# A routed-expert kernel: splitting one store, and working off two early tiles of the first expert instead of one

## The chip, the cores and the metric

The kernel runs on 1 core of a Trainium2 chip, as one launch. The metric is device microseconds (us) for one execution. The core has five engines that each work through their own instructions in order and wait for one another by semaphores: TensorE (PE, matrix products; PEld is its weight load), VectorE (DVE), ScalarE (ACT), GpSimd (POOL) and SyncE (SP). SP, ACT and POOL also issue DMA transfers, which 16 DMA engines carry out.

## The reference

Three layers follow each other, all in float32:

- Attention for 4 batches, 8 heads, head width 64, with 512 local and 32 global tokens per batch. Local queries see a window of 32 positions to either side and the global keys; global queries see everything. The result has 2176 rows (4 x 544) of 512 numbers.
- A dense layer on these rows: `h = x @ w_in` (512 to 2048), `relu(h)` squared, `@ w_out` (back to 512).
- A routed layer: a row is worked on if `x @ w_skip > 0`. It goes to one expert of 8, the `argmax` of `x @ w_gate`, and its result is `x + gate * (relu(x @ w1[e]) @ w2[e])`, with `gate` the softmax probability of that expert. `w1[e]` is 512 x 1024 and `w2[e]` 1024 x 512. Other rows are copied.

## The kernel before, in words

**Tokens.** The 2176 rows are worked in 17 tiles of 128: 16 tiles of local tokens, and a last tile that holds the global tokens of all four batches (32 rows each). A row of the dense layer's result goes twice to DRAM: to `out`, and to a scratch tensor `x2d` that carries the row's gate as a 513th number. `store` (line 551) does it. For a local tile both targets are one block of 128 rows. For the last tile the target is four blocks of 32 rows that lie 544 rows apart, and one DMA to each target writes all four.

**Routing.** `route` (line 573) takes a tile in five steps (between its `yield`s): transpose the rows on PE and copy them on ACT; split them in three bfloat16 parts (`thirds`, three DVE operations); logits on PE, then the arg max, a long run of small DVE operations, and an exponential on ACT; rank the tokens within their expert (PE and some fifteen DVE operations, of which the second writes the gate into the row; for the last tile the store is issued right behind it, from SP); write the token's row number into a table of slots with a PE product and a DVE addition. Each expert has 17 columns of 128 slots in that table, one column per tile of its tokens. `slot_rows` (line 756) turns columns of the table into the row numbers that `gather` (line 821) reads and the scatter at the end of an expert's tile writes.

**Closing.** Before the last three tiles are routed (14 of 17 done), the kernel takes column 0 of expert 0 as final: it converts that column and raises expert 0's count to at least 128 (lines 982 to 985), so that later tokens go to later columns.

**An expert's tile.** `gather` fetches 128 rows of `x2d` by an indirect DMA from POOL. `prepare` (line 827) transposes them on PE (4 transposes) and splits them in a high and a low part (ACT, DVE). `expert_tile` (line 833) then has ten steps: four with 6 products each for the hidden layer, the third of which also turns the first half of the hidden values (4 transposes on PE, a cast on ACT, a subtraction on DVE); four with 6 products each for the output, the first of which turns the second half; one DVE operation that scales and adds; and the scatter, an indirect DMA from POOL.

**Weights.** An expert's weights come in 8 parts of 512 KB. `fetch_expert` (line 775) issues a part's DMA from SP, or from ACT where told; `convert_expert` (line 787) splits it in two halves (a cast on ACT, a subtraction on DVE or POOL). Parts are fetched up to 13 ahead.

**The order.** All engines' programs are written in the order in which the Python code emits them. `TAIL` (line 41) is that order by hand for the end of the dense layer and the start of the experts:

- `T`: the next step of the dense layer's last tile. `r`, `s`, `t`: a routing step of the last two local tiles and of the tile of global tokens.
- `O`: gather for tile 0 of expert 0, from the closed column. `pEJ`, `gEJ`: prepare, gather for tile J of expert E.
- `X`: the next step of tile 0 of expert 0. `S`: all columns of the table are converted, the counts copied.
- `w`, `W`: fetch the next weight part, from SP or from ACT. `C`, `c`: convert the next part, with DVE or POOL for the low half.

Behind `TAIL` come two more gathers and the scatter of expert 0's tile 0 (lines 1039 to 1042). Then, for every expert, its tile 0 is emitted with the weight traffic of the next expert, the counts are read into registers on every engine, and `more` (line 1048) emits tiles 1 to 4 in nested branches that are entered if the count is large enough. Before a tile is worked in such a branch the gather of the tile behind it is issued, and it is prepared after the sixth step.

Of the kernel before, what the change touches and what calls it, by code (L numbers as in the profile page):

```python
# [11 lines left out]
I32 = mybir.dt.int32  # L12
U32 = mybir.dt.uint32
AF = mybir.ActivationFunctionType
ALU = mybir.AluOpType
# [23 lines left out]
"""  # L39

TAIL = """
    w T T r T r r s T T s T s W r w T T r T s C C T c s w T T T C W O W T c C W T p00 C w C T w W T W W X t C
    X t t C X t c X t w w S g01 g10 X w w X w w X w p01 p10 X X
"""

WARM = 8
# [3 lines left out]
def attention_ffn_routed_experts(  # L50
# [499 lines left out]

    def store(t, x2, queue):

        globals_of = [d.rearrange("(b s) d -> b s d", b=B)[:, 0:SG, :] for d in (x2d, out)]
        if t < NLT:
            b, tt = divmod(t, TPB)
            r0 = b * S + SG + tt * P
            queue.dma_start(x2d[r0:r0 + P, :], x2)
            queue.dma_start(out[r0:r0 + P, :], x2[:, 0:DM])
        if t in (0, NLT):

            queue.dma_start(globals_of[0], x2)
        if t == NLT:
            queue.dma_start(globals_of[1], x2[:, 0:DM])

    w27 = []

# [150 lines left out]
    def ffn_tile(t):  # L717

        xh, xl = xts.pop("g")
        acc = ps.tile([P, DM], F32, tag="x2", bufs=2, name=f"acc{t}")  # L720
        gs = []
        for fb in range(N5):
            h = ps.tile([P, 512], F32, tag="h", bufs=2, name=f"h{t}_{fb}")
            for k in range(KD):
                w = w_in_t[k, fb]
                nc.tensor.matmul(h, lhsT=xh[:, k, :], rhs=w[:, 0, :], start=(k == 0), stop=False)
                nc.tensor.matmul(h, lhsT=xh[:, k, :], rhs=w[:, 1, :], start=False, stop=False)
                nc.tensor.matmul(h, lhsT=xl[:, k, :], rhs=w[:, 0, :], start=False, stop=(k == KD - 1))
                if k == 1:
                    yield  # L730
            g = sb("vr", 6, [P, ROW], f"g{t}_{fb}")[:, 0:512]
            square_relu(g, h)
            gs.append(g)
            yield
        for fb in range(N5 + 1):
            if fb < N5:
                tr = pair(f"gtr{t}_{fb}")
                transposes(tr, gs[fb])
                gh = sb("vr", 6, [P, ROW], f"gh{t}_{fb}")[:, 0:512].rearrange("p (a k) -> p a k", a=4).bitcast(F32R)
                gl = sb("pT", 2, [P, 4, P], f"gl{t}_{fb}").bitcast(F32R)  # L740
                split(gh, gl, tr)
                gs[fb] = (gh, gl)
            if fb:
                gh, gl = gs[fb - 1]
                for z in range(4):
                    f = 4 * (fb - 1) + z
                    wh, wl = wout(f)
                    nc.tensor.matmul(acc, lhsT=gh[:, z, :], rhs=wh, start=(f == 0), stop=False)
                    nc.tensor.matmul(acc, lhsT=gh[:, z, :], rhs=wl, start=False, stop=False)
                    nc.tensor.matmul(acc, lhsT=gl[:, z, :], rhs=wh, start=False, stop=(f == KF - 1))  # L750
                    if z % 2:
                        yield
        outs["g"] = (t, copy_out(t, acc))


    def slot_rows(gi, si, c0, c1):

        t = table[:, c0:c1]
        tmp = sb("ohs", 1, [P, NSLOT], f"slots{c0}_{c1}")[:, c0:c1]
        nc.vector.tensor_scalar(out=gi, in0=t, scalar1=-1.0, scalar2=0.0, op0=ALU.add, op1=ALU.max)  # L760
        nc.vector.tensor_scalar(out=tmp, in0=t, scalar1=0.0, scalar2=BIG, op0=ALU.is_equal, op1=ALU.mult)
        nc.vector.scalar_tensor_tensor(out=si, in0=tmp, scalar=-1.0, in1=t, op0=ALU.add, op1=ALU.add)
# [58 lines left out]
    def gather(e, j, gi):  # L821
        nc.gpsimd.indirect_dma_start(  # L822
            out=gathered(e, j), out_offset=None, in_=x2d, in_offset=bass.IndirectOffsetOnAxis(ap=gi, axis=0),
            bounds_check=NTOK - 1, oob_is_err=False,
        )

    def prepare(e, j):
        tr = pair(f"etr_{e}_{j}")
        transposes(tr, gathered(e, j))
        x = prepared(e, j)  # L830
        split(x[:, 0], x[:, 1], tr)
# [66 lines left out]
    with tc.manual_schedule():  # L898
# [54 lines left out]
        warm(WARM)  # L953
        for what in SEQ.split():
            do(what)
        first_slots = const.tile([P, 1], I32, name="g0"), const.tile([P, 1], I32, name="s0")
        rest_on[0] = nc.gpsimd
        for j in range(2, NB):
            emit = attention_block(j + 1) if j + 1 < NB else None
            ra, rb = outs.pop(j - 1)  # L960
            route_gens = {"r": route(*ra), "s": route(*rb)}
            ffn, unit, routed = ffn_block(j), -1, 0
            for what in (ODD if j % 2 else EVEN).split():
                if what in "FE":
                    square_on[0] = nc.vector if what == "F" else nc.scalar
                    next(ffn)
                    unit += 1
                    if j < NB - 1:
                        continue
                    if unit == 4:  # L970
                        xts["g"] = tuple(sb(n, 2, [P, KD, BLK], f"{n}_g", F32R)[:, :, 0:P] for n in ("xh", "xl"))
                        split(*xts["g"], xgT)
                    if unit == 16:
                        for n in range(FIRST):
                            fetch_expert(n, nc.sync)
                elif what in route_gens:
                    next(route_gens[what])
                    routed += 1
                    if j == NB - 1 and routed == 10:


                        slot_rows(*first_slots, 0, 1)
                        nc.vector.tensor_scalar(
                            out=count[:, 0:1], in0=count[:, 0:1], scalar1=float(P), scalar2=None, op0=ALU.max
                        )
                elif what == "V":
                    do(what)
                elif emit and what not in "rs":
                    emit(what)
# [5 lines left out]
        def slot(idx, e, j):  # L995
            c = e * TPE + j
            return idx[:, c:c + 1]

        route_gens = dict(zip("rs", (route(*o) for o in outs.pop(NB - 1))))
        ffn, tile00 = ffn_tile(NLT), None  # L1000
        fetched, converted = [FIRST], [0]
        for what in TAIL.split():
            if what == "T":
                next(ffn, None)
            elif what == "X":
                if tile00 is None:
                    tile00 = expert_tile(0, 0, first_slots[1])
                next(tile00)
            elif what in "rst":
                if what not in route_gens:  # L1010
                    route_gens[what] = route(*outs["g"])
                next(route_gens[what])
            elif what in "Cc":
                convert_expert(converted[0], nc.vector if what == "C" else nc.gpsimd)
                converted[0] += 1
            elif what in "Ww":
                fetch_expert(fetched[0], nc.scalar if what == "W" else nc.sync)
                fetched[0] += 1
            elif what == "O":
                open_places()  # L1020
                gather(0, 0, first_slots[0])
            elif what == "S":
                slot_rows(gidx, sidx, 0, NSLOT)
                nc.vector.tensor_copy(cnt, count)
            elif what[0] in "gp":
                e, j = map(int, what[1:])
                gather(e, j, slot(gidx, e, j)) if what[0] == "g" else prepare(e, j)

        def work(e, u):

# [8 lines left out]
        for u in AHEAD:  # L1039
            for n, j in AHEAD[u]:  # L1040
                gather(n, j, slot(gidx, n, j))
        next(tile00, None)

        def hint(e, j):

# [25 lines left out]
        for e in range(E):  # L1071
            for u, _ in enumerate(expert_tile(e, 0, slot(sidx, e, 0)) if e else ()):
                if u == 0:
                    hint(e, 1)
                if u == U1:
                    prepare(e, 1)
                if u == U0 and e + 1 < E:
                    prepare(e + 1, 0)
                work(e, u)
            if n_tok is None:  # L1080
                n_tok = [
                    nc.values_load(
                        cnt[0:1, i:i + 1], min_val=0, max_val=NTOK,
                        skip_runtime_bounds_check_because="a count of tokens, from 0 to all of them",
                    )
                    for i in range(E)
                ]
            more(e, 1)


# [28 lines left out]
```

## Time and profile before

| what | value |
|---|---|
| median of 3 runs | 785.13 us (784.14 to 787.31) |
| profiled execution | 787.99 us, of which the span from first to last instruction 786.3 us |
| mean granted TensorE clock | 0.972 of full |
| PE busy | 745.4 us (95%) |
| DVE, ACT, POOL busy | 427.2 us (54%), 395.4 us (50%), 175.2 us (22%) |

All times of the profile are microseconds from the span's start. The profile's views used below are: stretches (busy time of each engine in a window, with the number of its instructions, the granted TensorE clock and the share of the 16 DMA engines that is busy); waits (an engine's waits by what ended them: sum, number, longest); the timeline of an engine (start, length, operation; in brackets the idle time before it and what ended it); the summary of one line; the SP queue's timeline (when DMAs were issued). Busy matmuls overlap, so a step from one start to the next is the time that a product costs. A line ending in q (SPq, ACTq) is the issuing of a DMA or another instruction of that engine's sequencer, not its work.

### The profile page before, as it was taken

The page shows a single profiled execution, that of the slowest core. Times are in us where ns is not written, and L with a number is a line of the kernel's source. Part 1 is how long each engine was busy: PE and PEld are TensorE (multiplying, and loading weights), DVE is VectorE, ACT ScalarE, POOL GpSimd, SP SyncE. Part 2 cuts the span into 40 slices and gives each one's busy share as a digit, 9 for nine tenths or more (in the row PEclk, how much of TensorE's full clock was granted, in tenths as well). Part 3 has the DMA queues.
Part 4 walks back from the last instruction along what each step waited for, and adds up shares of the span by engine and source line. Part 5 has one row for each costly group of instructions (what it writes and reads, how often), then busy time and mean ns, then how long its engine had stood idle before and what let it go on. Part 6 is the DMA issues. An engine that isn't in the chain of part 4 may idle for free. (4 is left out here: it accounts for less than half of the span.)

```text
span 786.3 us, 16840 instructions
## 1 busy us (share of the span) xinstructions
PE 745.4 (95%) x6547; PEld 613.7 (78%) x6547; DVE 427.2 (54%) x1109; ACT 395.4 (50%) x972; POOL 175.2 (22%) x211
## 2 busy tenths in 40 slices
PE   6889999999999999999999999999885999999897
PEld 4666677888888888888888888887654877887775
DVE  2877984954641641662552663332781178417882
ACT  5774665566345544544654543433360268426771
POOL 5000121231211112111211111221222133313421
PEclk8598999999999999999999999999998999999999
DMA  9899470250425024142313031002458179516700
GB/s 265 222 318 273 104 185 7 58 132 28 105 55 125 28 45 88 33 128 63 78 45 95 2 118 51 5 28 80 146 191 292 55 249 326 194 53 243 272 25 30
DMA packets 117270, 95.21 MB, mean 121 GB/s; under 512 B 83005, under 2 KB 90173, under 8 KB 117164
## 3 DMA queue, kind: packets, MB, share of 16 engines
q1 hardware_dynamic: 107640, 73.17, 33.1%
q10 hardware_dynamic: 6644, 12.33, 4.3%
q0 software_dynamic: 2880, 8.33, 3.1%
q8 instruction: 62, 1.02, 0.5%
q14 instruction: 44, 0.36, 0.1%
HBM read 82.08 MB, written 12.85 MB: 121 GB/s over the span
## 5 line engine op out<-in xcount | busy, mean ns | idle before, releaser
L178 POOL TENSOR_TENSOR gl<-g,gh 128x256 fp32r<-128x256 f32 x107 | 78.8, 736 | 343.0 <-ACT gh L177 191.4
L669 PE MATMUL h<-xh,w_in 128*128 128x256 f32 x448 | 131.7, 294 | 0.0
L671 PE MATMUL h<-xh,w_in 128*128 128x256 f32 x448 | 126.6, 283 | 0.0
L670 PE MATMUL h<-xl,w_in 128*128 128x256 f32 x448 | 126.3, 282 | 0.0
L673 ACT ACTIVATE g<-h 128x256 f32<-128x256 f32 x128 | 48.8, 381 | 105.8 <-PE h L671 66.3
L690 PE MATMUL acc<-w_out,gh 128*128 128x512 f32 x224 | 93.4, 417 | 0.0
L692 PE MATMUL acc<-w_out,gl 128*128 128x512 f32 x224 | 88.3, 394 | 0.0
L691 PE MATMUL acc<-w_out,gh 128*128 128x512 f32 x224 | 88.1, 393 | 0.0
L669 PEld LDWEIGHTS h<-xh,w_in 128*128 128x128 f32 x448 | 84.7, 189 | 3.5
L670 PEld LDWEIGHTS h<-xl,w_in 128*128 128x128 f32 x448 | 84.6, 189 | 1.8
L671 PEld LDWEIGHTS h<-xh,w_in 128*128 128x128 f32 x448 | 84.4, 188 | 0.0
L410 ACT ACTIVATE sm<-sm,mx 128x128 f32<-128x128 f32 x128 | 49.9, 391 | 61.7 <-DVE mx L408 59.2
L177 ACT CAST gh<-g 128x256 fp32r<-128x256 f32 x112 | 45.4, 406 | 25.9 <-DVE g L703 23.7
L703 DVE TENSOR_TENSOR g<-h,g 128x256 f32<-128x256 f32 x44 | 18.5, 420 | 58.1 <-ACT g L673 58.0
L692 PEld LDWEIGHTS acc<-w_out,gl 128*128 128x128 f32 x224 | 42.1, 188 | 10.0 <-POOL gl L178 0.2
L178 DVE TENSOR_TENSOR ehl<-ertr,ehl 128x512 fp32r<-128x512 f32 x28 | 19.4, 691 | 52.9 <-ACT ehl L177 52.9
L690 PEld LDWEIGHTS acc<-w_out,gh 128*128 128x128 f32 x224 | 42.2, 188 | 6.8 <-ACT gh L177 0.4
L691 PEld LDWEIGHTS acc<-w_out,gh 128*128 128x128 f32 x224 | 42.3, 189 | 5.7 <-issue 0.3
L853 ACT ACTIVATE er<-eh 128x512 f32<-128x512 f32 x28 | 16.7, 597 | 38.7 <-PE eh L850 38.7
L688 PE MATMUL acc<-st_raw_out,gh 128*128 128x512 f32 x64 | 33.6, 649 | 0.0
L822 POOL DMA_INDIRECT xg<-x2d,slots x21 | 23.5, 1121 | 43.7 <-DVE xp L178 8.6
L890 POOL DMA_INDIRECT out_dram<-eo,slots x13 | 16.5, 1269 | 71.5 <-DVE eo L886 39.7
(706 smaller groups left out, 1681.9 us busy)
## 6 DMA issues: line engine op xcount, KB each, us to landing
st_e<-in_moe_w_dram SPq DMA_DIRECT2D x57, 512.0 KB, 8.0
vr<-in_v_l_dram SPq DMA_DIRECT2D x56, 192.0 KB, 3.7
st_raw_in<-in_moe_w_in_dram SPq DMA_DIRECT2D x16, 512.0 KB, 7.3
st_raw_out<-in_moe_w_out_dram SPq DMA_DIRECT2D x16, 512.0 KB, 5.4
x2d<-x ACTq DMA_DIRECT2D x17, 256.5 KB, 2.8
st_gv<-in_v_l_dram SPq DMA_DIRECT2D x8, 512.0 KB, 6.8
out_dram<-x ACTq DMA_DIRECT2D x16, 256.0 KB, 3.0
st_e<-in_moe_w_dram ACTq DMA_DIRECT2D x7, 512.0 KB, 5.5
```

The lines of the kernel that those rows point to most:

```text
L177: nc.scalar.copy(hi, src)
L178: (lo_engine or nc.vector).tensor_tensor(out=lo, in0=src, in1=hi.bitcast(F32), op=ALU.subtract)
L410: nc.scalar.activation(sm[:, hh, :], sm[:, hh, :], AF.Exp, bias=mx[:, hh:hh + 1], scale=SCALE, accum_out=osum[:, 2 * hh + g:2 * hh + g + 1],)
L669: nc.tensor.matmul(h, lhsT=wh, rhs=xh[:, k, :], start=(k == 0), stop=False)
L670: nc.tensor.matmul(h, lhsT=wh, rhs=xl[:, k, :], start=False, stop=False)
L671: nc.tensor.matmul(h, lhsT=wl, rhs=xh[:, k, :], start=False, stop=(k == KD - 1))
L673: nc.scalar.activation(g, h, AF.Relu)
L688: nc.tensor.matmul(acc[z], lhsT=gh[:, c], rhs=w, start=(f == 0), stop=(f == KF - 1))
L690: nc.tensor.matmul(acc[z], lhsT=gh[:, c], rhs=wh, start=(f == 0), stop=False)
L691: nc.tensor.matmul(acc[z], lhsT=gh[:, c], rhs=wl, start=False, stop=False)
L692: nc.tensor.matmul(acc[z], lhsT=gl[:, c], rhs=wh, start=False, stop=(f == KF - 1))
L822: nc.gpsimd.indirect_dma_start(out=gathered(e, j), out_offset=None, in_=x2d, in_offset=bass.IndirectOffsetOnAxis(ap=gi, axis=0), bounds_ch ...
```

## The change

Three things change.

- `store`: the last tile's one DMA to `x2d` and one to `out` become four each, one per block of 32 rows, the four to `x2d` first.
- Two columns of expert 0 are closed in place of one (the count is raised to at least 256). `O` issues both gathers. A letter `Y` is new: a step of expert 0's tile 1. `p01` moves up to the end of the dense layer's last tile. All ten steps of tile 0 (`X`) stand between the routing steps of the last tile and right behind `S`; the steps of tile 1 (`Y`) follow. The branch for tile 1 is gone: `more` starts at tile 2 for expert 0.
- Behind `S` the gathers are those for tile 2 of expert 0 and tile 0 of expert 1; the scatter of tile 0 is issued behind them, inside `TAIL`. The seven last fetches of `TAIL`, which SP issued before, are issued by ACT, between the steps `Y`.

```diff
-    w T T r T r r s T T s T s W r w T T r T s C C T c s w T T T C W O W T c C W T p00 C w C T w W T W W X t C
-    X t t C X t c X t w w S g01 g10 X w w X w w X w p01 p10 X X
+    w T T r T r r s T T s T s W r w T T r T s C C T c s w T T T C W O W T c C W T p00 C w C T p01 w W T W W X X
+    t C X t X t C X X t c X X X t S g02 g10 X Y Y Y W W Y W W p02 p10 Y W W Y Y W Y Y Y Y
...
-        globals_of = [d.rearrange("(b s) d -> b s d", b=B)[:, 0:SG, :] for d in (x2d, out)]
...
-        if t in (0, NLT):
-
-            queue.dma_start(globals_of[0], x2)
+        if t == 0:
+
+            queue.dma_start(x2d.rearrange("(b s) d -> b s d", b=B)[:, 0:SG, :], x2)
         if t == NLT:
-            queue.dma_start(globals_of[1], x2[:, 0:DM])
+
+            for d, n in ((x2d, ROW), (out, DM)):
+                for b in range(B):
+                    queue.dma_start(d[b * S:b * S + SG, :], x2[b * SG:(b + 1) * SG, 0:n])
...
-                        slot_rows(*first_slots, 0, 1)
+                        slot_rows(*first_slots, 0, 2)
                         nc.vector.tensor_scalar(
-                            out=count[:, 0:1], in0=count[:, 0:1], scalar1=float(P), scalar2=None, op0=ALU.max
+                            out=count[:, 0:1], in0=count[:, 0:1], scalar1=2.0 * P, scalar2=None, op0=ALU.max
...
-            elif what == "X":
-                if tile00 is None:
-                    tile00 = expert_tile(0, 0, first_slots[1])
-                next(tile00)
+            elif what in "XY":
+                j = "XY".index(what)
+                if j not in early:
+                    early[j] = expert_tile(0, j, first_slots[1][:, j:j + 1])
+                next(early[j], None)
...
-                gather(0, 0, first_slots[0])
+                for j in range(2):
+                    gather(0, j, first_slots[0][:, j:j + 1])
...
-        next(tile00, None)
...
-            more(e, 1)
+            more(e, 1 if e else 2)
```

## Rows read from the trace of the kernel before

**Rows 1.** The page: PE busy in tenths, in 40 slices of the span.

```profile
PE   6889999999999999999999999999885999999897
```

**Rows 2.** Stretches: length, busy (instructions) of PE, PEld, DVE, ACT, POOL; clock, DMA share, GB/s.

```profile
595.00:600.00 5.00, 0.00 (x0) 0.00 (x0) 0.00 (x0) 0.00 (x0) 3.83 (x4) 0.94 1.03 388
...
646.50:660.00 13.50, 13.21 (x64) 10.52 (x64) 11.73 (x13) 11.03 (x15) 5.22 (x4) 1.00 0.99 334
```

**Rows 3.** Stretches, PE alone: length, busy (instructions); clock, DMA share, GB/s.

```profile
575.90:607.57 31.67, 18.85 (x85) 0.84 0.68 230
607.57:620.16 12.59, 12.59 (x60) 1.00 0.17 57
...
584.00:585.70 1.70, 1.70 (x8) 0.50 0.00 0
```

**Rows 4.** Waits of PE from 560 us on: sum, times, longest.

```profile
PE etr L272 <- DMA xg<-x2d,slots: 8.4, 2, 7.8
PE pt L645 <- DVE ohl L642: 3.7, 2, 1.9
...
PE pl L591 <- DVE x2T L570: 1.4, 1, 1.4
```

**Rows 5.** Timeline of PE: start, length, operation, [idle before, releaser].

```profile
574.07 0.60 PE L272 MATMUL etr<-ident,xg 128*128 128x128 f32 x4
574.42 0.48 PE L748 MATMUL acc<-w_out,gh 128*128 128x512 f32 x1
...
602.05 1.09 PE L272 MATMUL etr<-ident,xg 128*128 128x128 f32 x4 [7.78 <-DMA xg<-x2d,slots]
...
607.57 0.49 PE L848 MATMUL eh<-e0h,xp 128*128 128x512 f32 x1 [0.65 <-issue]
...
618.77 0.39 PE L863 MATMUL y<-e7h,ehl 128*128 128x512 f32 x1
...
620.16 0.39 PE L848 MATMUL eh<-e0h,xp 128*128 128x512 f32 x1
```

**Rows 6.** Timeline of the SP queue.

```profile
587.57 0.65 SPq L561 DMA_DIRECT2D x2d<-x  x1
...
588.96 47.23 SPq L785 DMA_DIRECT2D st_e<-in_moe_w_dram  x14
```

**Rows 7.** DMA queues from 589.5 to 590.5: packets, MB, share of 16 engines.

```profile
q1 hardware_dynamic: 9, 0.02, 25.5%
```

**Rows 8.** Lines 557 (store of a local tile) and 822 (gather), ns and us.

```profile
L557 ACTq DMA_DIRECT2D x2d<-x x16: 327/332/376, 158.5 to 562.2; - x16
DMA to landing us min/median/max: 2.6/2.8/3.1
...
DMA to landing us min/median/max: 3.5/4.2/6.9
```

**Rows 9.** Timeline of POOL.

```profile
595.25 1.01 POOL L822 DMA_INDIRECT xg<-x2d,slots  x1 [7.70 <-DMA x2d<-x]
...
607.99 1.02 POOL L890 DMA_INDIRECT out_dram<-eo,s  x1 [7.81 <-DVE eo L886]
612.08 1.03 POOL L822 DMA_INDIRECT xg<-x2d,slots  x1 [3.07 <-DMA out_dram<-eo,s]
```

**Rows 10.** Timeline of DVE, the last tile's routing.

```profile
587.15 0.14 DVE L618 TENSOR_SCALAR rt<-rt 128x1 f32<-128x1 f32 x1
...
588.86 0.34 DVE L642 TENSOR_SCALAR ohl<-iota_s,rt 128x128 fp32r<-128x128 f32 x1
...
589.96 0.23 DVE L760 TENSOR_SCALAR slots<-table 128x136 int32<-128x136 f32 x1
```

**Rows 11.** Issues of line 785 (weight fetches), ns, and SP's longest wait there, us.

```profile
L785 SPq DMA_DIRECT2D st_e<-in_moe_w_dram x57: 367/462/1542, 456.2 to 738.0; - x57
...
L785 ACTq DMA_DIRECT2D st_e<-in_moe_w_dram x7: 374/403/583, 557.0 to 576.5; - x7
...
SPq L785 <- PEq L1061: 71.0, 5, 37.9
```

More of the change, by code (lines that the diff above doesn't have):

```diff
@@ L955, in attention_ffn_routed_experts @@
             do(what)
-        first_slots = const.tile([P, 1], I32, name="g0"), const.tile([P, 1], I32, name="s0")
+        first_slots = const.tile([P, 2], I32, name="g0"), const.tile([P, 2], I32, name="s0")
         rest_on[0] = nc.gpsimd
@@ L999, in attention_ffn_routed_experts @@
         route_gens = dict(zip("rs", (route(*o) for o in outs.pop(NB - 1))))
-        ffn, tile00 = ffn_tile(NLT), None
+        ffn, early = ffn_tile(NLT), {}
         fetched, converted = [FIRST], [0]
@@ L1026, in attention_ffn_routed_experts @@
                 e, j = map(int, what[1:])
-                gather(e, j, slot(gidx, e, j)) if what[0] == "g" else prepare(e, j)
+                if what[0] == "g":
+                    gather(e, j, slot(gidx, e, j))
+                else:
+                    prepare(e, j)
         def work(e, u):
```

## The prediction

> **What bounds the kernel now.** I read the page's slices first: PE is at 9 tenths almost everywhere, with one dip of 8, 8, 5 in slices 29 to 31, about 570 to 610 us [rows 1]. The stretches place it: from 595 to 600 PE does nothing, while the DMA engines are fully busy (share 1.03); in the expert stage, for instance from 646.5 to 660, PE is busy 13.21 of 13.50 us at full clock although the DMA share is 0.99 there [rows 2]. So time can be won only in that dip, and what is won there should stay won, since behind it PE is the bound. The waits name the dip's causes: 8.4 us for two gathers of `x2d` (7.8 in one piece), 3.7 for the last routing's DVE chain (longest 1.9), 1.4 for `thirds` [rows 4].
>
> The stretch that the change rewrites runs from 575.90, where expert 0's tile 0 starts, to 620.16, where its tile 2 starts: 31.67 + 12.59 = 44.26 us [rows 3]. What PE has to do in it, I price from full-clock rows. Six products take 620.16 - 618.77 = 1.39 us; a group of four transposes 574.42 - 574.07 = 0.35 us [rows 5]. Two tiles are 96 products, 22.2 us; four turns, three prepares (0,1; 1,0; 0,2) and the last routing's transposes are 8 groups, 2.8 us; the routing's small products I estimate at 0.6 us. Sum 25.6 us. [...]
>
> Why the gather is late: SP issues the last tile's store at 587.57 [rows 6], and POOL's gather waits for it until 595.25, 7.68 us later [rows 9]. A local tile's store of the same size lands in 2.8 us [rows 8]. While the late one is all that moves, a quarter (25.5%) of the 16 engines is busy, so four carry it [rows 7]; and from 588.96 SP puts weight fetches behind it, 512 KB each [rows 6]. The gather then needs 602.05 - 595.25 = 6.8 us in that traffic against a median of 4.2 [rows 8, 9].
>
> **The change part by part.** *Nothing is added on PE*: both versions have the same 96 products and 8 groups in this stretch, in another order. I follow the new order, from PE's 575.9 on.
>
> *p01, X, X, t, X, t, X, t.* The gather for tile 1 sits behind the first one on POOL, about 1.0 us of POOL [rows 9], with nothing due; its data are there well before p01. PE: 0.35, twelve products 2.8, the routing's transposes 0.35, then a step with its turn, 1.4 + 0.35, and a step of 1.4: 582.6. `thirds` stands behind that turn's cast and subtraction on DVE and ends at about 584.8 by the order of the queue. PE waits 2.2 us, as it does now (1.4 + 0.5 in the rows). I keep the slow clock behind it too: 3.4 us at half, 1.65 us lost.
>
> *X, X, t, then X, X, X, t.* Two steps and a turn at the partly slow clock end at 589.9. The ranking chain takes from 587.15 to 588.86 + 0.34, 2.05 us [rows 10]. Now PE waits for it; then two steps (2.8 us) lie beside it, so the 1.9 us go. PE is through tile 0 at 592.8. The table's conversion (0.23 us to the row numbers) comes behind the chain, the scale-and-add and the table's addition, at about 594.2, against 590.2 now [rows 10]. A loss of 4 us on that side, which the next step must make good.
>
> *The store.* Its first DMA goes out at 590.0, 2.4 us later than now, because the chain is emitted later. Four issues of 0.33 us and 2.8 us to landing [rows 8] give 593.8, instead of 7.68 us from the issue. Bounds: 2.6 us behind the first issue, or all 7.68 again; I take the local store's rows, which have the same bytes and one block of rows per DMA. [...] Each new DMA is 64 KB. [...]
>
> *The gathers behind S.* The fetches that crowd them are moved behind four steps of tile 1, so I take 3.5 to 4.2 us from issue to landing [rows 8], not 6.8. Issued at 594.3 and 1.3 us later: data at 597.8 to 598.5 and 599.1 to 599.8. PE has four steps and a turn of tile 1 in between, 592.9 to 598.9. So tile 2's prepare doesn't wait, and expert 1's waits about 0.3 us. The 7.8 + 0.6 us and the slow clock behind them go.
>
> *The rest of tile 1.* Four steps and a turn, 5.9 us, to about 606. *The branch* comes once in either version, now before tile 2. Each engine reads eight counts there. I take 1.0 us, against 0.65, since less work stands queued on PE beside the reads. *The early scatter* is off PE's path: POOL has two gathers ahead of it and nothing that PE needs behind it. Behind it come tile 1's scatter, the two gathers that now stood ahead, and the counts. The gather for tile 3, which is prepared though not worked off, then starts about 5 us behind the scale-and-add, as tile 2's does now (607.99 to 612.08, and the wait of its scatter) [rows 9]. It is wanted 9 us into tile 2. Nothing, or up to 2 us.
>
> *Fetches from ACT.* Seven issues of 0.40 us [rows 11] stand between ACT's casts; beside 1.4 us steps they cost nothing at that price. At SP's longest, 1.54 us, they would. For this and the small gaps between engines I put 0.8 us.
>
> Sum of losses left: 2.2 + 1.65 + 0.3 + 1.0 + 0.8 = 5.95 us, say 6.0. The stretch takes 25.6 + 6.0 = 31.6 us instead of 44.26: 12.6 us less. The profiled execution would be 787.99 - 12.6 = 775.4. It lies 2.9 us above the median of the runs; I carry the difference over to the median, 785.13 - 12.6 = 772.5 us. Its own range: without the slow clock and the small losses 2.5 us better, with a longer `thirds` wait, a full wait at tile 3's gather and dearer issues 4 us worse, so 770 to 776.5.
>
> **The rivals.**
> - *The split store lands no earlier.* Eight DMAs cost what one costs: 590.0 + 7.68 = 597.7, the gathers land at 601.5 and 602.8. PE then idles 3.2 us at the first prepare and about 1 us at the second, and gets the slow clock again (1.7 us). Gain 12.6 - 5.9 = 6.7: 778.4 us. [...] Against: four busy engines explain the late landing by themselves [rows 7].
> - *ACT becomes the next wait.* If the seven issues cost 1.0 to 1.54 us each because the DMA queues are full, as they did for SP at the worst [rows 11], four of them delay the second half's cast by up to 4 us and PE falls idle in tile 1, with a slow clock behind: 5 us of the gain go, 777.5 us. Against: ACT's own seven took 0.37 to 0.58 us.
> - *The weights become the bound, slower than before.* The seven fetches start at about 598 instead of 588.96 [rows 6], 9 us later. If the stream of weights and not PE set the pace from 633 us on (its share is 0.99) [rows 2], all behind it would end 9 us later: 794 us. It decides where the low half of a part is not ready when its step comes. Against: SP waited up to 37.9 us to be let into the next expert's fetches [rows 11], so the stream has tens of microseconds of slack.
> - *The change adds a tile.* If fewer than 256 tokens of expert 0 were known when two columns are closed, the gap would be padding, and a fourth tile of 12.6 us [rows 3] would eat the gain: 785 us. Counting the reference's own choices on its inputs, 273 are known by then and 337 in all, 3 tiles either way.
>
> **How the numbers follow.** Forecast 0.72; store 0.09; ACT 0.10; weights 0.03; no net gain (an extra tile, or a stall that I haven't seen) 0.06. About 0.5% (3.9 us) is what a measurement can tell from no change. The first three cases are faster by more: 0.91. Same 0.06, slower 0.03. The range takes in the store's and the ACT's cases at the top and the missing slow clock at the bottom: 769.5 to 779.
>
> **What would show it.** In the new profile: PE without an idle time over 1 us between 585 and 606; the four store DMAs landing within 4 us of the first issue; gathers landing about 4 us behind their issue; tile 2's first product near 607. I am wrong if the wait for `xg` stays above 3 us, if ACT's casts end PE's waits in tile 1, or if the stage from 633 us on gets longer idle times at its weights.

## The result, and the profile after

| | median of the runs | lowest to highest |
|---|---|---|
| before | 786.22 us (4 runs) | 784.14 to 787.36 |
| after | 775.04 us (4 runs) | 773.36 to 777.68 |

After takes 0.987 of the time before (95% interval 0.9834 to 0.9905). The difference of the medians is 11.2 us; 12.6 was forecast, and 775.04 lies in the range. The profiled execution of after took 777.68 us (span 776.0) against 787.99 (span 786.3): 10.3 us less.

The 5 of [rows 1] is gone from PE's slices. The 7 in slice 29 (543 to 563 us) lies ahead of tile 0, at waits for the routing of earlier tiles that before has too. New is an 8 in slice 33, about 621 to 640 us:

```profile
PE   6899999999999999999999999999798989999897
```

Stretches of after, PE alone (columns as in [rows 3]). The first runs from the transposes of expert 0's tile 0 to the first product of its tile 2; the next are tile 2, expert 1, expert 2 and the first tile of expert 3, each up to the first product behind it:

```profile
572.78:606.98 34.20, 30.65 (x155) 0.95 0.56 191
606.98:620.36 13.38, 12.94 (x61) 1.00 0.53 180
620.36:636.14 15.78, 13.19 (x64) 1.00 0.91 315
636.14:651.16 15.02, 14.75 (x64) 0.89 0.85 285
651.16:664.18 13.02, 13.02 (x65) 1.00 0.92 310
```

The same stretches of before (the first takes in the 44.26 us of [rows 3]):

```profile
574.07:620.16 46.09, 33.27 (x154) 0.89 0.56 188
620.16:633.25 13.09, 12.65 (x61) 1.00 0.13 42
633.25:646.71 13.46, 13.20 (x65) 1.00 0.91 316
646.71:660.18 13.47, 13.20 (x64) 1.00 0.99 335
660.18:673.97 13.79, 13.30 (x65) 1.00 0.98 336
```

The first stretch fell from 46.09 to 34.20 us, by 11.9. Behind it 2.32 us are lost in expert 1 (15.78 against 13.46) and 1.55 in expert 2 (15.02 against 13.47, with the clock at 0.89); the next tile gives 0.77 back.

PE's waits in after from 560 us on, which stand against [rows 4]. The wait for `xg` is 0.6 us in place of 8.4, the routing's `ohl` 1.9 in place of 3.7 (the one left is an earlier tile's), and the waits for ACT's queue at the branch lines have grown from 1.1 us (4 times, longest 0.3) to 3.7 (5 times, longest 2.6):

```profile
PE eh L850 <- ACTq L1067: 3.7, 5, 2.6
PE pt L647 <- DVE ohl L644: 1.9, 1, 1.9
...
PE pl L593 <- DVE x2T L572: 1.3, 1, 1.3
...
PE eh L850 <- issue: 1.1, 1, 1.1
PE etr L272 <- DMA xg<-x2d,slots: 0.6, 1, 0.6
```

PE's timeline in after, against [rows 5]: the two waits for `thirds`, the prepares of tile 2 (none) and of expert 1 (0.62), the branch before tile 2, and the branch before expert 2 (line 1067 reads the counts there):

```profile
583.03 0.19 PE L593 MATMUL pl<-w,x2T 128*128 128x27 bf16 x1 [1.31 <-DVE x2T L572]
...
583.76 0.41 PE L593 MATMUL pl<-w,x2T 128*128 128x27 bf16 x10 [0.54 <-DVE x2T L573]
...
598.00 0.60 PE L272 MATMUL etr<-ident,xg 128*128 128x128 f32 x4
...
599.22 0.63 PE L272 MATMUL etr<-ident,xg 128*128 128x128 f32 x4 [0.62 <-DMA xg<-x2d,slots]
...
606.98 0.50 PE L850 MATMUL eh<-e0h,xp 128*128 128x512 f32 x1 [1.08 <-issue]
...
636.14 0.65 PE L850 MATMUL eh<-e16h,xp 128*128 128x512 f32 x1 [2.60 <-ACTq L1067]
```

SP's queue in after, against [rows 6]: the four DMAs to `x2d`, then the four to `out`; SP's next weight fetch comes at 597.74, not 588.96:

```profile
588.53 1.75 SPq L565 DMA_DIRECT2D x2d<-x  x4
590.32 1.84 SPq L565 DMA_DIRECT2D out_dram<-x  x4
```

POOL in after, against [rows 9]. The first gather no longer waits for the store but for the row numbers; the store's last block had landed at 591.8:

```profile
593.54 1.09 POOL L824 DMA_INDIRECT xg<-x2d,slots  x1 [4.20 <-DVE slots L763]
594.94 1.00 POOL L824 DMA_INDIRECT xg<-x2d,slots  x1 [0.30 <-issue]
596.24 1.03 POOL L892 DMA_INDIRECT out_dram<-eo,s  x1 [0.30 <-issue]
```

ACT's queue in after, the seven fetches (0.45 to 0.59 us each in the mean of a row, against [rows 11]):

```profile
596.80 0.90 ACTq L787 DMA_DIRECT2D st_e<-in_moe_w_dram  x2
...
598.21 1.18 ACTq L787 DMA_DIRECT2D st_e<-in_moe_w_dram  x2
...
601.74 1.42 ACTq L787 DMA_DIRECT2D st_e<-in_moe_w_dram  x3
```

### The profile page after: what moved, and what is told of

Read it like the earlier page. It is cut to its first block, busy times and chain, and to the rows that moved or that the text cites. A ratio compares the mean times of both kernels' runs of the same rounds, so it can differ in the third digit from the quotient of the medians.

```text
span 776.0 us, 16823 instructions
## 1 busy us (share of the span) xinstructions
PE 743.4 (96%) x6547; PEld 613.6 (79%) x6547; DVE 427.4 (55%) x1109; ACT 395.5 (51%) x972; POOL 179.8 (23%) x211
## 5 line engine op out<-in xcount | busy, mean ns | idle before, releaser
L824 POOL DMA_INDIRECT xg<-x2d,slots x20 | 25.4, 1271 | 39.6 <-DVE xp L178 16.7
L707 ACT ACTIVATE g<-g 128x256 f32<-128x256 f32 x68 | 28.7, 422 | 5.8 <-DVE rt L625 1.5
```

Of the source, the lines that this page charges most:

```text
L707: nc.scalar.activation(square, g, AF.Square)
```

## The experiments

"Stretch" below runs from tile 0's transposes to tile 2's first product: before 46.09 us, after 34.20 (34.09 when repeated). That measure is better than the whole time for telling causes apart, since in the profiles tile 0 started anywhere from 567.6 to 574.9 us, although the kernels differ little up to there. Each stretch is read from one profile.

| kernel | median us (runs) | before beside it | ratio, 95% | stretch us |
|---|---|---|---|---|
| split store alone | 782.67 (12) | 785.97 | 0.9945 (0.9921 to 0.9968) | 43.16 |
| two early tiles, one store | 784.42 (12) | 785.97 | 0.9977 (0.9948 to 1.0006) | 41.60 |
| fetches ahead of `S` | 783.57 (12) | 785.97 | 0.9963 (0.9939 to 0.9987) | 41.43 |
| one store and fetches ahead of `S` | 786.10 (12) | 785.97 | 1.0008 (0.9981 to 1.0035) | 44.76 |
| scatter first | 784.90 (12) | 786.35 | 0.9974 (0.9950 to 0.9999) | 41.78 |
| one store, late fetches | 783.45 (12) | 784.53 | 0.9980 (0.9960 to 1.0001) | 40.00 |
| after again | 774.46 (4) | 784.75 | 0.9874 (0.9854 to 0.9894) | 34.09 |
| ACT shifted by 64 | 777.27 (6) | 784.75 | 0.9913 (0.9892 to 0.9934) | 34.40 |
| ACT shifted by 24 | 776.47 (6) | 784.75 | 0.9904 (0.9885 to 0.9924) | 34.18 |
| `thirds` ahead | 774.86 (6) | 784.75 | 0.9880 (0.9858 to 0.9902) | 31.68 |
| `thirds` ahead, ACT shifted | 773.43 (6) | 786.35 | 0.9840 (0.9812 to 0.9869) | 31.69 |

**The split store alone**, in the kernel before.

```diff
...
-            queue.dma_start(globals_of[0], x2)
...
-            queue.dma_start(globals_of[1], x2[:, 0:DM])
...
+            for d, n in ((x2d, ROW), (out, DM)):
+                for b in range(B):
+                    queue.dma_start(d[b * S:b * S + SG, :], x2[b * SG:(b + 1) * SG, 0:n])
```

> The kernel before with the last tile's store split in eight, and nothing else. Theory (four engines made the store late): the store lands about 3.3 us behind its issue at 587.6 instead of 7.7, the gather starts near 591.5 instead of 595.25, still amid the weight fetches, so PE's wait of 7.8 us shrinks to about 4: 782.5 us, 3.7 less than before. Rival (the weight fetches right behind the store made it late): the store lands as late as before, 786 us.

Measured: 782.67, 3.3 us less than before. POOL's gather no longer waits for the store (its releaser is the last count, on DVE), and PE's wait is 3.80 us where [rows 5] has 7.78:

```profile
588.28 1.01 POOL L824 DMA_INDIRECT xg<-x2d,slots  x1 [3.79 <-DVE cnt L1026]
```

```profile
595.01 0.63 PE L272 MATMUL etr<-ident,xg 128*128 128x128 f32 x4 [3.80 <-DMA xg<-x2d,slots]
```

What is left is the gather itself, 6.7 us amid fetches, with nothing for PE beside it. The forecast of this run, 782.5, held.

**After, with one store per target.**

```diff
-                for b in range(B):
-                    queue.dma_start(d[b * S:b * S + SG, :], x2[b * SG:(b + 1) * SG, 0:n])
+                queue.dma_start(d.rearrange("(b s) d -> b s d", b=B)[:, 0:SG, :], x2[:, 0:n])
```

> The changed kernel with the last tile's store as one DMA to each target again. Theory (four engines): landing 7.7 us behind the issue at 588.5, that is 596.2 instead of 591.8; the gathers start 2.7 us later than in the changed kernel, PE waits 2.5 to 3 us for the first and gets a slow clock behind it: 779 us. Rival (the fetches behind it made it late, and here there are none): it lands by 593.5, where the slot numbers are ready anyway: 775 us, no difference.

Measured: 784.42, no gain over before that these runs can tell (interval up to 1.0006). The store was issued at 588.11 with no weight fetch behind it, and the gather waited for it until 595.30, 7.2 us. So the late landing needs no fetches behind it, and that rival falls. While only the two stores moved, the busy share was 23.0%, near the quarter of [rows 7]; with the split it was 59.4% (first this run from 590 to 594, then after from 590 to 591.5):

```profile
q1 hardware_dynamic: 134, 0.27, 23.0%
```

```profile
q1 hardware_dynamic: 156, 0.22, 59.4%
```

The same queue carries the store to `out`, issued 0.7 us behind. At 0.27 MB in 4 us the two stores, 0.525 MB, take 7.8 us, an estimate; how long the one to `x2d` would take by itself was not run. The price of the late landing was larger than expected, 7.4 us of stretch:

```profile
595.30 1.01 POOL L823 DMA_INDIRECT xg<-x2d,slots  x1 [6.95 <-DMA x2d<-x]
```

```profile
601.17 1.09 PE L272 MATMUL etr<-ident,xg 128*128 128x128 f32 x4 [3.97 <-DMA xg<-x2d,slots]
...
604.18 1.09 PE L272 MATMUL etr<-ident,xg 128*128 128x128 f32 x4 [1.92 <-DMA xg<-x2d,slots]
```

```profile
600.50:607.33 6.83, 4.24 (x14) 0.50 0.97 360
```

Counted from the stretch's start the gathers start 2.7 us later than in after (595.30 - 571.80 = 23.50, against 593.54 - 572.78 = 20.76). They then share the DMA engines with ACT's fetches: from issue to data 5.9 and 7.6 us. PE waits 5.89 us in place of 0.62, that is 5.3 of the 7.4. The last fence shows the rest: PE had stood idle since 597.20, and from 600.50 on it got the lower clock level (0.50) for 6.83 us.

**After, with the fetches ahead of `S`, and this together with one store per target.**

```diff
-    ... X X X t S g02 g10 X Y Y Y W W Y W W p02 p10 Y W W Y Y W Y Y Y Y
+    ... X X X t W W W W W W W S g02 g10 X Y Y Y Y p02 p10 Y Y Y Y Y Y Y
```

> The changed kernel with the seven last weight fetches, still issued by ACT, ahead of S and its gathers instead of between the steps of tile 1. Theory (crowding): the gathers take 6.8 us instead of about 4, PE waits 2.5 to 3.5 us at the two prepares: 778.5 us. Rival (the wait of 2.6 us before expert 2 in the changed kernel comes from weights that were fetched 9 us later): that wait and the slow clock behind it go, and the time is 772 us.

> The changed kernel with one store DMA per target and with the seven fetches ahead of S: of the change, the two early tiles alone are left. Theory (store and crowding add up): landing near 596, gathers 6.8 us behind it, so PE waits 4 to 5 us and gets a slow clock: 781 us, less than half of the change's gain. Rival (the second tile's work alone covers the gather): 776 us.

Measured: 783.57 and 786.10. With the split store, ACT issued from 586.91, ahead of the store, and its last five issues took 8.71 us:

```profile
587.85 8.71 ACTq L787 DMA_DIRECT2D st_e<-in_moe_w_dram  x5
```

```profile
595.85 1.01 POOL L824 DMA_INDIRECT xg<-x2d,slots  x1 [6.86 <-DMA x2d<-x]
```

The split store, issued at 588.55, held the gather until 595.85, and one of PE's turns waited 1.33 us for ACT. So both runs were dearer than expected (778.5 and 781) for a reason that the expectations lack: fetches ahead of the store delay the store, not only the gather (7.3 us from its issue, against 3.3 in after). With the single store it is worst, 11.9 us from its issue at 589.46:

```profile
601.37 1.01 POOL L823 DMA_INDIRECT xg<-x2d,slots  x1 [11.93 <-DMA x2d<-x]
```

PE waits 8.95 us for it. With one store and the fetches in this place the early tile is therefore worth nothing that can be measured (ratio 1.0008); the split by itself is worth 3.3 us, the whole change 11.2. The early tile with the fetches where before has them, issued by SP behind the store, was not run. The fetches ahead of `S` did not take away the wait before expert 2 (2.2 us there), so late weights aren't its cause.

**The scatter ahead of the gathers.**

```diff
-    ... X X X t S g02 g10 X Y Y Y W W ...
+    ... X X X t S X g02 g10 Y Y Y W W ...
```

> The changed kernel with tile 0's scatter ahead of the two gathers behind S instead of behind them. Theory (POOL works its indirect DMAs in order, about 1.3 us each, and the scatter also waits for the stores to out): the first gather starts 1.3 to 1.5 us later, PE waits 1 to 2 us longer at the two prepares: 776 us. Rival (the scatter's place does not matter): 774.5 us, the wait for xg stays near 0.5 us.

Measured: 784.90; 776 was expected. On POOL the scatter takes its turn, and the gathers start 1.3 us apart behind it, the first 2.2 us later from the stretch's start than in after (597.78 - 574.85 = 22.93, against 20.76):

```profile
596.45 1.03 POOL L892 DMA_INDIRECT out_dram<-eo,s  x1 [5.04 <-DVE cnt L1028]
597.78 1.04 POOL L824 DMA_INDIRECT xg<-x2d,slots  x1 [0.31 <-issue]
599.13 1.01 POOL L824 DMA_INDIRECT xg<-x2d,slots  x1 [0.30 <-issue]
```

```profile
601.37 0.63 PE L272 MATMUL etr<-ident,xg 128*128 128x128 f32 x4 [1.13 <-DMA xg<-x2d,slots]
...
607.07 1.09 PE L272 MATMUL etr<-ident,xg 128*128 128x128 f32 x4 [5.07 <-DMA xg<-x2d,slots]
```

Of the 2.2 us the scatter's turn makes 1.3. The 2.2 us go with 7.6 us more of stretch. The first gather still arrives in 3.6 us; the second, which falls among the fetches, needs 7.9. PE waits 6.2 us, and the lower clock follows (0.50 from 605 to 610 us). The order "gathers ahead of the early scatter" thus carries as much of the stretch as the split does within the changed kernel (7.4).

**One store, the fetches behind both prepares.** This asks whether the single store's price is the collision with the fetches.

```diff
-    ... S g02 g10 X Y Y Y W W Y W W p02 p10 Y W W Y Y W Y Y Y Y
+    ... S g02 g10 X Y Y Y Y p02 p10 Y W W W Y W W Y W W Y Y Y Y
```

> The changed kernel with one store DMA per target again, and the seven weight fetches all behind the two prepares. In the kernel with one store the gathers started 2 us later and took 5.9 and 7.6 us, amid the fetches that ACT issues from tile 1's third step on. Theory (a late gather costs what it is late, and the rest of that kernel's loss is the collision with the fetches and the slow clock behind it): gathers take about 4 us, PE waits 1 to 2.5 us, and from tile 0's prepare to tile 2's first product 36 to 37 us instead of 41.6; 778 us. Rival (the late store alone costs it): the stretch stays near 41 us, 784 us.

Measured: 783.45, stretch 40.00; 36 to 37 was expected. Only 1.6 of the 7.4 us were the collision, so that expectation fell:

```profile
600.14 0.63 PE L272 MATMUL etr<-ident,xg 128*128 128x128 f32 x4 [1.82 <-DMA xg<-x2d,slots]
...
603.14 1.09 PE L272 MATMUL etr<-ident,xg 128*128 128x128 f32 x4 [2.37 <-DMA xg<-x2d,slots]
```

```profile
601.24:608.07 6.83, 4.93 (x16) 0.50 0.32 115
```

The waits are 4.2 us in place of 0.6, and the clock of the last row makes most of the other 2.2 us. The gathers start 3.05 us later from the stretch's start than in after (596.73 - 572.92 = 23.81), and that costs nearly 6 us even without ACT's fetches. One fetch of SP's, issued at 598.48, still falls beside the gathers (3.4 and 5.1 us to data).

**The wait before expert 2.** In after ACT's work stands still at the branch line (1067) for 2.62 us. PE's next product waits for the semaphore that ACT raises on that line, not for work of ACT's: it starts at 636.14, ahead of ACT's next cast:

```profile
636.34 1.04 ACT L795 CAST e19h<-st_e 128x1024 fp32r<-128x1024 f32 x1 [2.62 <-ACTq L1067]
```

The change added issues to ACT's program, so that everything behind them stands at other places of it. The test adds copies of one column, which compute nothing that is used, early in ACT's program (64, then 24):

```diff
+                    steps[0] += 1
+                    if steps[0] % 3 == 0 and steps[0] <= 3 * SHIFT:
+                        nc.scalar.copy(idle2[:, 0:1], idle2[:, 1:2])
```

> The changed kernel with 64 tiny ACT copies (128x1, on a tile of its own) spread over the dense layer, one behind every third step, so that all later ACT instructions lie 64 places further on. Theory (at the branch behind expert 1, ACT waits for its instructions, which depends on where they lie): ACT's branch there takes 1.5 us instead of 3.8, PE's wait of 2.6 us goes, and with it up to 1.6 us of slow clock: 771 to 773 us, unless another branch gets such a wait. Rival (ACT or the weights are behind with their work there): the wait stays at 2 us or more, 775 us.

> As the one with 64 ACT copies, but 24 of them. Theory (place of the instructions): the length of ACT's branch behind expert 1 differs between 0, 24 and 64 copies, being near 1.5 us or near 3.8 us. Rival: it is the same in all three, and so is the time, 775 us.

Measured: PE's wait there is 0.27 us with 24 copies and at most 0.3 with 64, and expert 1's stretch is back at its length before (13.48 us with 24, before 13.46). With 24 copies, PE's first product of expert 2, ACT, and then the stretches of experts 1 to 3:

```profile
635.87 0.50 PE L850 MATMUL eh<-e16h,xp 128*128 128x512 f32 x1 [0.27 <-ACTq L1073]
```

```profile
637.13 1.05 ACT L795 CAST e19h<-st_e 128x1024 fp32r<-128x1024 f32 x1 [1.36 <-POOL e17l L801]
```

```profile
622.39:635.87 13.48, 13.21 (x64) 1.00 0.91 318
635.87:649.34 13.47, 13.20 (x65) 1.00 0.98 334
649.34:663.25 13.91, 13.30 (x65) 1.00 1.01 341
```

That the branch's cost changes with what stands ahead of it in ACT's program is shown: PE's longest wait for ACT's queue at that line is 2.0 to 2.7 us in the eight profiles with the new order and no copies, and 0.3 in before, the split alone and the three profiles with copies. From ACT's branch instruction (632.26) to the next one of its sequencer (636.08) the trace of after has 3.82 us, that of before 1.49 (645.15 to 646.64). What ACT waits for is not shown directly. The DMA rows have transfers of instructions inside the standstill of after (632.7 to 636.1 us):

```profile
q8 instruction: 1, 0.02, 2.1%
q14 instruction: 2, 0.02, 1.5%
```

An 8 KB transfer on q14 starts 1.94 us behind the branch (634.20, for 0.39 us), and ACT goes on 1.49 us behind its end. In before no transfer of instructions starts between the branch and ACT's going on. The rows don't say for which engine a transfer is, so that ACT fetched code there remains an inference.

The whole time did not fall with it: 777.27 and 776.47, where 771 to 773 was expected of the first, against 774.46 for after beside them. Part of what is won at the branch comes back as waits for converted weights. With 24 copies PE waits 0.6 us for `e25l` and 1.1 for `e58l`, with 64 0.7 and 1.1; before waits for both (0.5 and 1.1), after for neither. So from tile 2's first product to the end the profiles take 166.2 and 167.2 us with copies, against 169.0 and 167.1 in the two of after. How much the copies themselves take ahead of tile 0 isn't settled: its start scatters more (574.50 and 567.62, against 572.78 and 570.36).

**`thirds` ahead**, and with ACT shifted by 24 copies (three behind each of the first eight steps of the dense layer's last tile).

```diff
-    t C X t X t C X X t c X X X t S ...
+    t C t X X t C X X t c X X X t S ...
```

> The changed kernel once more, to have its time beside the next three and beside more runs of the kernel before: 775 us, 11 us less than before, with the same wait of PE of about 2.6 us at the branch ahead of expert 2.

> The changed kernel with the last tile's second routing step (the split in three parts on DVE) emitted ahead of tile 0's third step instead of behind it. Theory (thirds waits in DVE's order behind the turn's subtraction, PE waits for it and then runs at the lower clock): the waits of 1.3 and 0.5 us before the logits go, and the slow clock at 585 us with them, 1.8 to 3.5 us less: 772 us. Rival (the turn's subtraction then comes later and PE waits for it at the next output step): 775 us.

> The kernel with the split in thirds ahead of tile 0's third step, and 24 tiny ACT copies at the first eight steps of the dense layer's last tile, where ACT idles. Theory (both effects are separate and add): from tile 0's prepare to tile 2's first product 31.7 us instead of 34.2, and ACT's branch behind expert 1 1.5 us instead of 3.8; 3 to 5 us less than the changed kernel, that is 770 to 772 beside 774.5. Rival (the weights' conversion behind expert 2 takes the gain back): the stretch is shorter but the time is 774.

Measured: after again has 774.46, with PE's wait before expert 2 at 2.55 us, as expected. With `thirds` emitted ahead of the `X` that held it up, PE's waits of 1.31 and 0.54 us and the lower clock behind them go (1.00 in the whole stretch): the stretch is 31.68 us, 2.5 less than after, as expected. The time stays (774.86, where 772 was expected), since the wait before expert 2 is 2.73 us there and the lower clock comes behind it (0.50 for 6.83 us). With ACT shifted too, the median is 773.43, the lowest of all (770 to 772 was expected), and the clock stays at its upper level in the stretch and in expert 1:

```profile
572.53:604.22 31.69, 29.49 (x154) 1.00 0.68 227
617.59:631.04 13.45, 13.19 (x64) 1.00 0.92 319
```

Its ratio to before is 0.9840, that of after 0.9874, and the two intervals overlap: it beats before clearly; that it beats the changed kernel these runs don't prove.

## Why the prediction was right, step by step

- **The sum.** From where tile 0's steps begin, tile 1's prepare with them: 31.6 us forecast, 32.35 measured (574.63, when that prepare starts, to 606.98). That the two are so near is in part luck. PE's work was priced at 25.6 us, which is 2 too little: the same products and transposes keep it busy for 27.65 us where the clock is at its upper level throughout (`thirds` ahead, ACT shifted, 574.37 to 604.22). The 96 products take 24.0 us there, not 22.2: the ten that stand behind transposes or routing products cost 0.3 us each in place of 0.23, and three ahead of an idle time 0.4. The eight groups take 3.15, not 2.8. Against that, other terms were too large. In after PE is busy for 28.80 us, so the lower clock costs 1.15, not 1.65; it is idle for 3.55, which are the four waits below, and nothing is left for the 0.8 us of small gaps. The same work stands in the kernel before: of its 44.26 us, 16.6 were losses, not the 18.7 that 25.6 us of work would leave.
- **`thirds`.** 2.2 us of waiting forecast, 1.85 measured. The lower clock behind it was forecast at 1.65 us lost, 3.4 us at half; before has it so (0.51 from 582.35 to 585.75), and in after it comes (0.50 from 585.13 to 588.55) and costs 1.15. It isn't sure to come: in the kernel with 24 copies PE has the same two waits (1.31 and 0.54), and its clock stays at 1.00 in the whole stretch.
- **The ranking chain's wait of 1.9 us.** It went (in after PE has no wait for `ohl` between 565 and 622 us): two steps of tile 0 lie beside the chain.
- **The store.** 3.8 us to landing forecast, 3.3 measured (588.53 to 591.8). The rival of the split that lands no earlier falls: the four DMAs of 64.1 KB to `x2d` landed in 3.3 us, the single one in 7.2. The busy shares, 23.0% with the single DMAs and 59.4% with the split, say that the split put more engines to work; what decides how many a DMA gets was not shown.
- **The price of a late store.** This term was too small: 5.9 us in the rival, 7.4 in the run. The rival had waits of 4.2 us (its own times, 601.5 and 598.9, give 2.6 at the first prepare and not 3.2); 5.9 came, and the lower clock lasted 6.83 us. The rival has no collision of the late gathers with ACT's fetches.
- **The gathers.** 3.5 to 4.2 us forecast. The first was there when PE came, 4.46 us behind its issue; the second took 4.3, and PE waited 0.62 us against 0.3.
- **The branch.** 1.0 forecast, 1.08 measured.
- **ACT's issues.** 0.40 us each forecast, 0.37 to 0.76 measured, and no PE wait for ACT in tile 1. The rival that ACT becomes the wait falls for this order. With the fetches ahead of `S` ACT does hold PE up (1.33 us), while five issues take 8.71 us of its queue (see the last section). Why SP's issues are dear at times isn't shown: in before one took 1.54 us at a DMA share of 0.93 (646.9 to 648.6) and one 1.12 at 0.58 (712.6 to 713.9).
- **The weights as the bound.** This falls: the fetches start at 596.80, 8 us later than in [rows 6], and SP still waits up to 38.6 us to be let into the next expert's. The extra tile falls too, as the products show: PE has 6547 matmuls in both profiles.
- **"What is won there should stay won."** This step failed. Of the 13.18 us that after leads at tile 2's first product (620.16 - 606.98; 1.29 of them from an earlier start of the stretch), 10.3 are left at the end. At the branch before expert 2 PE waits 2.60 us for ACT, and gets the lower clock for 3.42 us behind it (0.50 from 636.33 to 639.75). The repeated profile has the same wait (2.55 us) and loses 1.0 us there, not 2.9, so the size of the loss varies. I had taken PE as the only bound behind the stretch, and had not priced that a shift of ACT's program changes a branch.

The forecast carried a gain of 12.6 us; 11.9 came in its stretch, and 11.2 in the medians.

## What to carry to other kernels

Here DMAs of four blocks of rows kept about a quarter of the engines busy (25.5% in before, 23.0% with one store in the new order), and blocks of 64.1 KB, each a DMA of its own, landed in 3.3 us in place of 7.2; where a consumer waits for such a transfer, try that. The parts of a change need not add: the split alone gave 3.3 us, the early tiles with one store 1.5 that can't be told from nothing, the whole change 11.2. Price a chain of dependent transfers by what PE has left to do at its end: here 2 to 3 us of delay (store, scatter, fetches) cost 6 to 8 us of stretch, since the next gather meets other traffic (DMA share 0.97 from 600.50 on in the run with one store) and the clock falls behind the wait (0.50 for 6.83 us there). An edit to one engine's program can move a wait into a branch far behind it (2.60 us here, 0.27 with 24 copies), so compare the stages behind the change as well as the one that was edited.

## What the runs showed that I had not expected

- The same branch cost PE 2.60 us or 0.27, by 24 small instructions more in ACT's program.
- Five 512 KB fetches issued in a row from ACT took 8.71 us of its queue, and 3.77 us in the kernel with the single store. What held them no view of these runs names. In the trace of after the split store's blocks and ACT's next fetches raise the same semaphores (110, 101, 103 and 104), so a wait for one of them is my guess.
- The split alone is worth 2.9 us of stretch, the early tile alone (with the fetches ahead of `S`) 1.3, the whole change 11.9.
- DVE's `rt` (line 625, 128 x 8 numbers) took 1.00 us at 588.37, while POOL ran a 128 x 1024 subtraction from 586.95 to 589.35, and ended 0.02 us behind it; in before it took 0.17. No run takes POOL's operation away.
